# One level of Winograd's scheme in a GEGLU feed-forward kernel: two pairs of f tiles share one run of plain bf16 products

## The chip, the cores and the metric

The kernel runs on one core of one Trainium2 chip. The metric is the device time of one execution in microseconds (us). Three runs of the kernel before took 539.51, 539.78 and 540.17 us; the median is 539.78 us.

TensorE (PE in the profile) multiplies a stationary 128x128 block with a moving 128x512 block and writes to PSUM, which here is used as eight banks of 128x512 f32. VectorE (DVE) and ScalarE (ACT) read and write those banks; GpSimd (POOL) forms sums in SBUF; SyncE (SP) and ScalarE's queue issue the DMAs.

## The reference

```python
B, S, D, F = 1, 2048, 1024, 3584          # all bf16
def reference(x, w_gate, w_up, w_down):
    return (_gelu(x @ w_gate) * (x @ w_up)) @ w_down   # gelu: tanh approximation
```

## The kernel before

The 2048 tokens are done in two halves of 1024. In each half a gate-and-up stage computes `hT`, the transposed product gelu(gate) times up, for all 28 tiles of 128 columns of F; then a down stage multiplies it with `w_down`. A half's tokens are two blocks of 512, held transposed as `xT[0]` and `xT[1]`. This page is about the gate-and-up stage; the down stage (`down_group`, L681) is left as it is.

**Seven products.** Two f tiles form a pair (14 pairs a half). For gate (j = 0) and up (j = 1) each, a pair is a 2x2 block product: weights `a(i, kh)` (f tile i, half kh of D) times x blocks `b(kh, l)` (half kh of D, token block l). Winograd's form needs seven products instead of eight. Two are *plain*: M1 = a(0,0) b(0,0) and M2 = a(0,1) b(1,0), with operands in bf16 straight from the loaded weights and from `xT`. The other five have sums as operands, in fp32r: M5 = s1 t1, M6 = s2 t2, M7 = s3 t3, M3 = s4 b22, M4 = a22 t4. The x sums t1 to t4 are formed once a half (`t_sum`, L241). The weight sums s1 to s4 are formed for every pair, eight of them with gate and up, by POOL (`s_sum`, L364; L385 is the instruction), and `a22` is a cast by ACT (L398). One product is four matmuls (`mm`, L410, instruction at L413), since half of D is four blocks of 128. So a pair is 16 plain matmuls and 40 fp32r ones.

**Banks.** The eight banks are four sets of two (gate and up): PB, VB, QB, RB. M1 goes to one set and ACT copies it to QB (L468); M2 is added to M1 and the pair's first output (f tile 0, tokens 0) is ready: gelu by ACT (`gelu`, L283) and multiplication by DVE (`mult`, L288). M6 is added to the copy of M1 in QB and copied by ACT to RB (L464). M5 goes to the fourth set and is copied by ACT to SBUF (`m5`, L458). DVE adds m5 to QB (`add_m5`, L436), and, when M7 has been added to RB, writes RB plus m5 to M5's set; then M3 is added in QB and M4 in RB. Each of these three sets ends in a gelu and a `mult`.

**Order.** Every engine's order is the order of the program text, fixed by hand (`on`, L110). `pair_quads` (L405) does one pair. It begins with M1; M2 is put on the list `pending` (L403) and is done behind M1 of the *next* pair (L473), so that the plain products of one pair and the next stand together. The last pair of a half does its own M2 at once too. Then come M6, M6, M5, M5 (gate, up each), M7, M3, M4. M1's set alternates between PB and VB (L445). Because M5 of pair p reads s1, and so on, the sums for pair p + 1 are written in place behind the products that read those of pair p (`prep`, L427): POOL starts them when M5 of gate is done, and they are next read by M6 of pair p + 1.

**Work that rides along**, through the dict `then` and the calls of `done`: in the first half, 42 "stage steps" of VectorE (`stage_step`, L619, instruction at L630) form the sums of `w_down` that the down stage needs later and store them to DRAM; each 3 steps need one tile of `w_down` (`stage_load`, L612, three buffers `wd_sb`). Four steps go to a pair: two behind M4's `mult` in DVE's order, and two behind the next M2's `mult`. Also x for the second half is transposed by DMA (`stage_x`, L641), and the next weights, one chunk of gate and one of up for two pairs, are loaded from ACT's queue (`load_w`, L155), gate behind M1, up behind M3. Rows of `w_down` for the down stage are loaded by SP into the weights' memory (`load_wd_rows`, L549, and `load_b22`, L552) at the last two pairs. The DMA semaphores are taken in turn, eight of them, so a DMA also waits until the one eight places before it has landed.

Pair 0 of the first half is done without the scheme (`first_pair_units`, L326); pair 1 of the first half does its M1 and M2 together and forms t4 meanwhile (`eager`, L470).

Of the kernel before, what the change touches and what calls it, by code (L numbers as in the profile page):

```python
# [34 lines left out]
def kernel(  # L35
# [8 lines left out]
    nc = tc.nc  # L44
# [355 lines left out]
    S_NAMES = ("s1", "s2", "s3", "s4", "a22")  # L400


    pending = []  # L403

    def pair_quads(hT, h, pair, nxt, then):  # L405

        key = (h, "p", pair)
        f0 = 2 * pair

        def mm(bank, j, lhs, rhs, start):  # L410
            for c in range(KH):
                pe(
                    nc.tensor.matmul(  # L413
                        banks[bank][:],
                        lhsT=lhs[:, c, :],
                        rhs=rhs[:, c, :],
                        start=start and c == 0,
                        stop=c == KH - 1,
                        skip_group_check=True,
                    )  # L420
                )

        def done(name):
            for f in then.get(name, ()):
                f()

        def prep(j, name):  # L427
            if nxt is not None:
                s_sum(nxt[0], nxt[1], j, name)

        def s(j, name):
            return ssum[(h, pair, j, name)]

        def add_m5(dst, src):
            dve(
                nc.vector.tensor_tensor(  # L436
                    out=banks[dst][:], in0=banks[src][:], in1=m5[j][:], op=ALU.add
                )
            )

        b11 = xT[0][:, half(0), :]
        b21 = xT[0][:, half(1), :]
        m5 = [None, None]
        g = {}
        P_, V_ = (PB, VB) if pair % 2 == 0 else (VB, PB)  # L445

        def m2():
            for j in range(2):
                mm(P_[j], j, block(key, j, 0, 1), b21, False)
                if j == 0:  # L450
                    g[0] = gelu(banks[P_[0]], nxt is None)
                else:
                    mult(hT, g[0], banks[P_[1]], f0, 0)

        def do_m5(j):
            mm(V_[j], j, s(j, "s1"), tsum["t1"], True)
            m5[j] = m_pool.tile([P, TB], F32, name=f"m5_{j}")
            act(nc.scalar.copy(out=m5[j][:], in_=banks[V_[j]][:]))  # L458
            if not eager:
                prep(j, "s1")  # L460

        def do_m6(j):
            mm(QB[j], j, s(j, "s2"), tsum["t2"], False)
            act(nc.scalar.copy(out=banks[RB[j]][:], in_=banks[QB[j]][:]))  # L464

        for j in range(2):
            mm(P_[j], j, block(key, j, 0, 0), b11, True)
            act(nc.scalar.copy(out=banks[QB[j]][:], in_=banks[P_[j]][:]))  # L468
        behind = len(pending) > 0
        eager = not behind and "m2" in then  # L470
        if behind:

            pending.pop()()  # L473
        done("m2 of last")
        if behind:
            if nxt is None:
                m2()
                done("m2")
            else:
                pending.append(m2)  # L480
            order = (do_m6, 0), (do_m6, 1), (do_m5, 0), (do_m5, 1)
        elif eager:
            m2()
            done("m2")
            order = (do_m5, 0), (do_m5, 1), (do_m6, 0), (do_m6, 1)
        else:
            pending.append(m2)
            order = (do_m5, 0), (do_m6, 0), (do_m6, 1), (do_m5, 1)
        for f, j in order:
            f(j)  # L490
            if (f, j) == (do_m6, 1):
                done("m6")
        for j in range(2):
            add_m5(QB[j], QB[j])
            if not eager:
                prep(j, "s2")
        done("m5")
        if eager:
            pool_behind_dve()
            for name in ("s1", "s2"):  # L500
                for j in range(2):
                    prep(j, name)
        for j in range(2):
            mm(RB[j], j, s(j, "s3"), tsum["t3"], False)
            add_m5(V_[j], RB[j])
            prep(j, "s3")
            if j == 0:
                g[1] = gelu(banks[V_[0]], nxt is None)
            else:
                mult(hT, g[1], banks[V_[1]], f0 + 1, 1)  # L510
        done("m7")
        for j in range(2):
            mm(QB[j], j, s(j, "s4"), tsum["b22"], False)
            prep(j, "s4")
            if j == 0:
                g[2] = gelu(banks[QB[0]], nxt is None)
            else:
                mult(hT, g[2], banks[QB[1]], f0, 1)
        done("m3")
        for j in range(2):  # L520
            mm(RB[j], j, s(j, "a22"), tsum["t4"], False)
            prep(j, "a22")
            if j == 0:
                g[3] = gelu(banks[RB[0]], nxt is None)
            else:
                mult(hT, g[3], banks[RB[1]], f0 + 1, 0)

        done("m4")

    SEQ = ("t1", "t2", "t3", "b22", "t4")
# [345 lines left out]

    for h in range(NH):
        hT = hT_pool.tile([P, KF, SH], BF16, name="hT")
        first_pair = 0
        if h == 0:
            first_pair_units(hT)
            first_pair = 1
            xs = [(tb, kd) for tb in (1, 0) for kd in range(KD)]
            new_x(1)
            stage_load(0)  # L890
            stage_load(1)
        for pair in range(first_pair, NPAIR):
            then = {}
            if pair % PPG == 0 and (pair // PPG + 1) * PPG < NPAIR:
                key = (h, pair // PPG + 1)

                if key not in chunks:
                    new_chunk(key)
                    for j, at in enumerate(("m2 of last", "m3")):
                        then[at] = [lambda j=j: load_w(key, j, 0, KD, act)]  # L900
            if h == 0 and pair < PPG:
                then = {
                    "m2": [lambda j=j: s_sum(0, pair, j, "a22") for j in range(2)]
                    + [lambda: t_sum("t4", 0, KH // 2)],
                    "m5": [lambda: t_sum("t4", KH // 2, KH)],
                }
            if h == 0 and pair >= PPG:

                n = [min(4 * (pair - PPG + d), NSTEP) for d in range(3)]
                steps = [lambda k=k: stage_step(k) for k in range(n[0], n[1])]  # L910
                new = range((n[1] + 2) // 3, (n[2] + 2) // 3)

                then["m2 of last"] = (
                    then.get("m2 of last", [])
                    + steps[:2]
                    + [lambda q=q: stage_x(hT, *q) for q in xs[:2]]
                )
                then["m7"] = [store_x] + [lambda i=i: stage_load(i) for i in new]
                then["m4"] = steps[2:]
                xs = xs[2:]  # L920
            if pair == NPAIR - 2:

                then.setdefault("m2 of last", []).extend(
                    [lambda: load_wd_rows(0, 4), lambda: load_wd_rows(4, 8)]
                )
            if 6 < pair < 11:
                i = 2 * pair - 8
                then.setdefault("m6", []).append(
                    lambda i=i: s_down(hT, 0, "s3", i, i + 2)
                )  # L930
            if pair == NPAIR - 1:
                then |= {
                    "m2 of last": [
                        lambda: load_b22(4, NS),
                        lambda: early.append(
                            wd_pool.tile([P, WDT, D], BF16, name="wd_sb")
                        ),
                        lambda: s_down(hT, 0, "s3", 0, 4),
                    ],
                    "m6": [  # L940
                        lambda: s_down(hT, 0, "s1", 4, 8),
                        lambda: t_down(0, "t1", 4, 6),
                    ],
                    "m2": [
                        lambda: load_wd_rows(8, 10),
                        lambda: load_wd_rows(10, 12),
                        lambda: load_wd_rows(12, NS),
                        lambda: load_b22(0, 4),
                    ],
                    "m7": [lambda: s_down(hT, 0, "s1", 0, 4)],  # L950
                    "m3": [lambda: t_down(0, "t1", 0, 2)],
                    "m4": [
                        lambda: t_down(0, "t2", 0, NT2),
                        lambda: t_down(0, "t1", 2, 4),
                        lambda: t_down(0, "t1", 6, 8),
                        lambda: s_down(hT, 0, "s1", 8, NS),
                        lambda: t_down(0, "t1", 8, NS),
                    ],
                }
            pair_quads(  # L960
                hT, h, pair, (h, pair + 1) if pair + 1 < NPAIR else None, then
            )

        then0 = {"m5": [lambda: s_down(hT, 0, "s3", 4, 6)]}
        then1 = {}
# [75 lines left out]
```

## Time and profile before

| what | value |
|---|---|
| median of three runs | 539.78 us |
| span of the profiled execution, first to last instruction | 538.0 us |
| median less span (work around the span) | 1.8 us |
| PE busy | 532.4 us, 99% of the span |
| DVE busy | 364.2 us, 68% |
| ACT busy | 263.5 us, 49% |
| POOL busy | 244.4 us, 45% |
| granted TensorE clock | full in every slice |
| gate and up, first half | about 19.6 to 183.2 us |
| gate and up, second half | about 271 to 447 us |
| one pair in the steady part | 12.56 us |

Busy time is the union of an engine's instructions. Matmuls overlap each other in the records (one lasts 0.38 to 0.39 us, and the next starts some 0.22 us later), so the pace is read from starts, not from durations. Of each run of plain products one record is missing (15 of 16 are listed).

### The profile page before, as it was taken

How to read it: one execution, taken by the hardware profiler on the slowest of the kernel's cores; microseconds unless marked ns; L12 is line 12 of the kernel's file. 1: busy time of each engine (PE TensorE's matmuls, PEld its weight loads, DVE VectorE, ACT ScalarE, POOL GpSimd, SP SyncE). 2: the span in 40 equal slices, each digit the busy share in tenths (PEclk: the TensorE clock that was granted, in tenths of full speed). 3: DMA queues.
4: the chain of work that ended last, by engine and by line, in shares of the span. 5: the costliest groups of instructions: out<-in, count | busy, mean ns of one | idle time of the engine just before them, and what ended most of it. 6: DMA issues, size and time to landing. Idle time of an engine off the chain costs nothing.

```text
span 538.0 us, 7084 instructions
## 1 busy us (share of the span) xinstructions
PE 532.4 (99%) x2352; PEld 377.9 (70%) x2388; DVE 364.2 (68%) x476; ACT 263.5 (49%) x447; POOL 244.4 (45%) x212
## 2 busy tenths in 40 slices
PE   9999999999999999999999999999999999999997
PEld 4577776666776686777776677777777766866866
DVE  1988777788775997989574334444444469969861
ACT  2555555555555329117465555555555552462280
POOL 0699877777776000000056776666777730000000
PEclk9999999999999999999999999999999999999999
DMA  9946876785815977789950405041322448677846
GB/s 205 323 128 195 207 252 185 238 262 197 291 61 200 361 239 246 237 279 308 324 171 1 156 1 158 15 142 57 100 78 80 155 133 284 220 246 252 293 141 212
DMA packets 92547, 102.70 MB, mean 191 GB/s; under 512 B 18656, under 2 KB 67424, under 8 KB 92512
## 3 DMA queue, kind: packets, MB, share of 16 engines
q1 hardware_dynamic: 69568, 80.23, 46.0%
q10 hardware_dynamic: 22944, 22.02, 13.4%
q8 instruction: 19, 0.31, 0.2%
q14 instruction: 16, 0.13, 0.1%
HBM read 85.98 MB, written 12.58 MB: 183 GB/s over the span
## 4 chain that ended last, share of the span: by engine, by line
PE 99%; issue 0%; ACT 0%; ACTq 0%
PE bank L413 63%; PE bank L703 33%; PE bank L264 3%; PE bank L202 1%; PE bank L308 0%; ACT bank L468 0%; ACT o_sb L759 0%; ACTq L468 0%
## 5 line engine op out<-in xcount | busy, mean ns | idle before, releaser
L413 PE MATMUL bank<-t_mem,s_mem 128*128 128x512 f32 x1056 | 249.6, 394 | 0.0
L413 PEld LDWEIGHTS bank<-t_mem,s_mem 128*128 128x128 f32 x1056 | 198.1, 188 | 44.1 <-DVE bank L436 0.4
L385 POOL TENSOR_TENSOR s_mem<-w_mem 128x512 fp32r<-128x512 bf16 x102 | 120.3, 1201 | 190.7 <-DVE t_mem L259 102.8
L703 PE MATMUL bank<-t_mem,s_mem 128*128 128x512 f32 (+1 forms) x548 | 127.2, 391 | 0.0
L288 DVE TENSOR_TENSOR hT<-w_mem,bank 128x512 bf16<-128x512 f32 x104 | 71.3, 687 | 79.9 <-PE bank L413 45.7
L703 PEld LDWEIGHTS bank<-t_mem,s_mem 128*128 128x128 f32 x548 | 102.4, 188 | 22.1 <-issue 0.2
L436 DVE TENSOR_TENSOR bank<-bank,m 128x512 f32<-128x512 f32 x108 | 69.9, 694 | 45.2 <-ACT m L458 43.7
L413 PE MATMUL bank<-xT,w_mem 128*128 128x512 bf16 x405 | 96.5, 380 | 1.4
L283 ACT ACTIVATE w_mem<-bank 128x512 f32<-128x512 f32 x104 | 61.8, 596 | 52.9 <-DVE bank L436 35.8
L413 PEld LDWEIGHTS <-w_mem 128*128 128x128 bf16 x432 | 40.2, 98 | 51.6 <-issue 6.8
L385 POOL TENSOR_TENSOR s_mem<-w_mem,s_mem 128x512 fp32r<-128x512 bf16 x52 | 65.8, 1285 | 0.0
L605 DVE TENSOR_TENSOR t_mem<-w_mem 128x1024 fp32r<-128x1024 bf16 x56 | 65.6, 1219 | 0.0
L385 POOL TENSOR_TENSOR s_mem<-s_mem,w_mem 128x512 fp32r<-128x512 f32 x52 | 60.9, 1192 | 0.0
L464 ACT COPY bank<-bank 128x512 f32<-128x512 f32 x54 | 30.8, 570 | 38.9 <-PE bank L413 38.9
L398 ACT CAST s_mem<-w_mem 128x512 fp32r<-128x512 bf16 x54 | 33.1, 615 | 30.6 <-PE bank L413 29.1
L675 DVE TENSOR_TENSOR s_mem<-hT 128x512 fp32r<-128x512 bf16 x52 | 34.2, 686 | 10.2 <-PE bank L703 9.4
L458 ACT COPY m<-bank 128x512 f32<-128x512 f32 x54 | 31.8, 589 | 17.5 <-PE bank L413 17.5
L703 PEld LDWEIGHTS <-hT 128*128 128x128 bf16 x224 | 21.3, 98 | 26.6 <-issue 2.1
L468 ACT COPY bank<-bank 128x512 f32<-128x512 f32 x54 | 30.7, 570 | 12.7 <-PE bank L413 12.7
L630 DVE TENSOR_TENSOR o_sb<-wd_sb,o_sb 128x512 fp32r<-128x512 bf16 x28 | 31.5, 1126 | 0.5
L768 ACT CAST o_sb<-bank 128x512 bf16<-128x512 f32 x27 | 14.8, 585 | 33.9 <-PE bank L703 33.9
L602 ACT CAST t_mem<-w_mem 128x1024 fp32r<-128x1024 bf16 x28 | 26.9, 1048 | 0.0
(45 smaller groups left out, 238.6 us busy)
## 6 DMA issues: line engine op xcount, KB each, us to landing
t_mem<-t_dram SPq DMA_DIRECT2D x56, 512.0 KB, 5.2
w_mem<-in_w_gate_dram ACTq DMA_DIRECT2D x10, 1024.0 KB, 5.5
w_mem<-in_w_up_dram ACTq DMA_DIRECT2D x10, 1024.0 KB, 5.5
wd_sb<-in_w_down_dram SPq DMA_DIRECT2D x28, 256.0 KB, 4.5
t_dram<-o_sb SPq DMA_DIRECT2D x28, 256.0 KB, 2.4
wd_sb<-in_w_down_dram SPq DMA_DIRECT2D x12, 512.0 KB, 7.7
w_mem<-in_w_down_dram SPq DMA_DIRECT2D x4, 1024.0 KB, 6.6
w_mem<-in_w_down_dram SPq DMA_DIRECT2D x8, 512.0 KB, 8.3
```

The source lines that it names most:

```text
L283: act(nc.scalar.activation(out=g_sb, in_=ps[:], func=ACT.Gelu_apprx_tanh))
L288: nc.vector.tensor_tensor(out=hT[:, fc, tb * TB : (tb + 1) * TB], in0=g_sb, in1=ps[:], op=ALU.mult,)
L385: pool(nc.gpsimd.tensor_tensor(out=t, in0=in0, in1=in1, op=op))
L398: act(nc.scalar.copy(out=t, in_=a(1, 1)))
L413: nc.tensor.matmul(banks[bank][:], lhsT=lhs[:, c, :], rhs=rhs[:, c, :], start=start and c == 0, stop=c == KH - 1, skip_group_check=True,)
L436: nc.vector.tensor_tensor(out=banks[dst][:], in0=banks[src][:], in1=m5[j][:], op=ALU.add)
L458: act(nc.scalar.copy(out=m5[j][:], in_=banks[V_[j]][:]))
L464: act(nc.scalar.copy(out=banks[RB[j]][:], in_=banks[QB[j]][:]))
L605: dve(nc.vector.tensor_tensor(out=t, in0=in0, in1=in1, op=ALU.subtract))
L630: dve(nc.vector.tensor_tensor(out=t, in0=in0, in1=in1, op=ALU.subtract))
L675: dve(nc.vector.tensor_tensor(out=t, in0=in0, in1=in1, op=op))
L703: nc.tensor.matmul(banks[bank][:, c0:c1], lhsT=lhs(i, u), rhs=rhs(i)[:, c0:c1], start=start and i == 0, stop=stop and i == NS - 1, skip_gr ...
```

## The change

`pair_quads` becomes `quads`, which does two pairs (a couple) at a time: M1 of both, then M2 of both, one run of 32 plain matmuls; then the five fp32r products of the first pair, and straight behind them those of the second. `pending` is gone. In the run the first pair uses PB with its copy in QB, the second RB with its copy in VB. After it M5 always goes to PB, RB takes the copy of M6, and M6 and M3 use QB for the first pair and VB for the second. Pair 1 of the first half is alone, in the old order, with VB for M1 and M2.

Of the work that rides along, VectorE's stage steps of a couple go four behind M1, two behind the M2s, one behind M3 of either pair (eight a couple, as before); the place behind M1 is ahead of the M2s' `mult` in VectorE's order. The tiles of `w_down` are loaded as soon as the steps leave a buffer free, at the start of a pair and behind M7, and three of them at first instead of two. Gate weights are loaded behind the M2s instead of behind M1. The order M5, M6, M6, M5 stays for the first couple of the second half alone. The loads of rows 8 to 13 of `w_down` and of the b22 blocks go to the start of the last pair.

```diff
-    def pair_quads(hT, h, pair, nxt, then):
+    def quads(hT, h, members, nxt, thens, m5_first):
+        last = nxt is None
+        run = []
+        for n, pair in enumerate(members):
+            after = (h, members[n + 1]) if n + 1 < len(members) else nxt
+            first_ = (PB, RB)[n] if len(members) > 1 else VB
+            run.append((pair, after, thens[n], first_, (QB, VB)[n]))
...
-        P_, V_ = (PB, VB) if pair % 2 == 0 else (VB, PB)
...
+        for pair, _, _, first_, q_ in run:
             for j in range(2):
+                mm(first_[j], block((h, "p", pair), j, 0, 0), b11, True)
+                act(nc.scalar.copy(out=banks[q_[j]][:], in_=banks[first_[j]][:]))
+        done(0, "m1")
+        for pair, _, _, first_, _ in run:
+            for j in range(2):
+                mm(first_[j], block((h, "p", pair), j, 0, 1), b21, False)
                 if j == 0:
+                    g = gelu(banks[first_[0]])
                 else:
+                    mult(hT, g, banks[first_[1]], 2 * pair, 0)
+        V_, R_ = PB, RB
+        for n, (pair, after, then, _, Q_) in enumerate(run):
...
+            done(n, "start")
+            if eager:
+                order = (do_m5, 0), (do_m5, 1), (do_m6, 0), (do_m6, 1)
+            elif m5_first and n == 0:
+                order = (do_m5, 0), (do_m6, 0), (do_m6, 1), (do_m5, 1)
             else:
+                order = (do_m6, 0), (do_m6, 1), (do_m5, 0), (do_m5, 1)
...
+        def run_steps(n):
+            for k in steps[:n]:
+                stage_step(k)
+            del steps[:n]
+        def run_loads():
+            while loads and 3 * (loads[0] - 2) <= NSTEP - len(steps):
+                stage_load(loads.pop(0))
...
+        for lead in range(begin, NPAIR, PPG):
+            members = range(lead, lead + PPG)
...
+                for j, at in enumerate(("start", "m3")):
+                    add(0, at, lambda j=j, key=key: load_w(key, j, 0, KD, act))
+            if h == 0:
+                add(0, "m1", lambda: run_steps(4))
+                add(0, "start", lambda: run_steps(2))
+                for n in range(PPG):
+                    add(n, "start", run_loads, run_x)
+                    add(n, "m7", store_x, run_loads)
+                    add(n, "m3", lambda: run_steps(1))
...
+                add(
+                    n,
+                    "start",
+                    lambda: load_b22(4, NS),
+                    lambda: load_wd_rows(8, 10),
+                    lambda: load_wd_rows(10, 12),
+                    lambda: load_wd_rows(12, NS),
+                    lambda: load_b22(0, 4),
                 )
...
+            quads(hT, h, members, nxt, thens, lead == 0)
```

## The prediction

> **What bounds the kernel now.** First the page's busy times and the two largest TensorE groups:
>
> ```profile
> PE 532.4 (99%) x2352; PEld 377.9 (70%) x2388; DVE 364.2 (68%) x476; ACT 263.5 (49%) x447; POOL 244.4 (45%) x212
> ...
> L413 PE MATMUL bank<-t_mem,s_mem 128*128 128x512 f32 x1056 | 249.6, 394 | 0.0
> ...
> L413 PE MATMUL bank<-xT,w_mem 128*128 128x512 bf16 x405 | 96.5, 380 | 1.4
> ```
>
> TensorE is never idle in gate and up (0.0 and 1.4 us, the latter beside missing records). The number of matmuls stays the same, so only their pace and new waits of TensorE can move the time. Next, the pace, from TensorE's timeline around three steady pairs (start, length, what, count):
>
> ```profile
> 131.28 3.63 PE L413 MATMUL bank<-xT,w_mem 128*128 128x512 bf16 x15
> 134.55 9.44 PE L413 MATMUL bank<-t_mem,s_mem 128*128 128x512 f32 x40
> 143.84 3.63 PE L413 MATMUL bank<-xT,w_mem 128*128 128x512 bf16 x15
> 147.11 9.44 PE L413 MATMUL bank<-t_mem,s_mem 128*128 128x512 f32 x40
> 156.40 3.63 PE L413 MATMUL bank<-xT,w_mem 128*128 128x512 bf16 x15
> ```
>
> and from two windows of it that lie inside a plain and inside an fp32r run:
>
> ```profile
> 131.94 2.32 PE L413 MATMUL bank<-xT,w_mem 128*128 128x512 bf16 x10
> ```
>
> ```profile
> 136.81 6.51 PE L413 MATMUL bank<-t_mem,s_mem 128*128 128x512 f32 x28
> ```
>
> A pair takes 143.84 - 131.28 = 12.56 us. Inside a run the step is (2.32 - 0.38)/9 = 0.2157 us for a plain matmul and (6.51 - 0.39)/27 = 0.2267 us for an fp32r one. Sixteen and forty make 3.451 + 9.068 = 12.519 us. The remaining **0.041 us is what one change from fp32r to plain and back costs**; no engine's wait is in it. Rounding (0.005 us in 6.51, times 40/27) leaves it between 0.03 and 0.05.
>
> Then the engines that TensorE could have to wait for: GpSimd's and VectorE's timelines.
>
> ```profile
> 137.73 2.29 POOL L385 TENSOR_TENSOR s_mem<-w_mem 128x512 fp32r<-128x512 bf16 x2 [3.07 <-PE bank L413]
> 139.98 2.31 POOL L385 TENSOR_TENSOR s_mem<-s_mem,w_mem 128x512 fp32r<-128x512 f32 x2
> 142.25 2.29 POOL L385 TENSOR_TENSOR s_mem<-w_mem 128x512 fp32r<-128x512 bf16 x2
> 144.50 2.73 POOL L385 TENSOR_TENSOR s_mem<-w_mem,s_mem 128x512 fp32r<-128x512 bf16 x2
> 150.29 2.29 POOL L385 TENSOR_TENSOR s_mem<-w_mem 128x512 fp32r<-128x512 bf16 x2 [3.06 <-PE bank L413]
> ```
>
> ```profile
> 156.84 0.69 DVE L288 TENSOR_TENSOR hT<-w_mem,bank 128x512 bf16<-128x512 f32 x1 [1.30 <-ACT w_mem L283]
> 157.44 1.33 DVE L630 TENSOR_TENSOR o_sb<-wd_sb,o_sb 128x512 fp32r<-128x512 bf16 x1
> 158.69 1.64 DVE L630 TENSOR_TENSOR o_sb<-wd_sb 128x512 fp32r<-128x512 bf16 x1
> 160.26 0.67 DVE L288 TENSOR_TENSOR hT<-w_mem,bank 128x512 bf16<-128x512 f32 x1
> 160.85 1.40 DVE L630 TENSOR_TENSOR o_sb<-wd_sb,o_sb 128x512 fp32r<-128x512 bf16 x2
> ```
>
> GpSimd's eight sums (s1, s2, s3, s4, gate and up) take 9.5 us a pair and end 3.4 us into the next run (144.50 + 2.73 - 143.84). A stage step takes 0.7 us (1.40 for two) where GpSimd rests and 1.33 to 1.64 us where it works.
>
> **The change, part by part.** I lay one couple out from the start of its run, with 0.863 us a plain product and 0.907 us an fp32r one: M1s end at 0.86, 1.73, 2.59, 3.45; M2s at 4.32, 5.18, 6.04, 6.92; the first pair's M6, M6, M5, M5 at 7.83, 8.74, 9.64, 10.55, its M7s at 11.46 and 12.36, M3s at 13.27 and 14.18, M4s at 15.08 and 15.99; the second pair's M6s begin at 15.99 and 16.90, its M5s end at 18.71 and 19.62, its M7s begin at 19.62 and 20.52, its M3s at 21.43 and 22.34; the couple ends at 25.06. ACT starts some 0.25 us behind a product, and its copy takes 0.57, its m5 copy 0.59, its gelu 0.60; DVE's `mult` and `add_m5` take 0.69 (rows of L468, L458, L283, L288, L436).
>
> *Fewer runs.* Before, there is a run for each of 13 pairs of the first half and 14 of the second: 27. After, it is 1 + 6 and 7: 14. Thirteen changes less at 0.041 give **-0.53 us**. Bounds: 0.05 gives -0.65; were the loss tied to the pairs and not to the change of type, 0.
>
> *Banks.* The second pair's M1 writes RB at 1.73 and 2.59; RB's last readers are the gelu and `mult` of the M4s just before. The `mult` row above ends 1.13 us behind the run's start (157.53 - 156.40), and the gelu comes ahead of it: 1.4 us to spare. M2 adds to a bank that is being copied: copy done at 1.73, M2 at 3.45. The copy of M6 (up) into RB must wait for the second M2's `mult`, below. M5 into PB at 8.74 and 9.64 needs the gelu and `mult` of M2s that end at about 5.2 and 6.2. Second pair: the copies of M6 into RB need M4's gelu and `mult` (17.3) and end at 17.8 and 18.6, for M7s at 19.62 and 20.52. Nothing: 0; the least cover is 1.4 us.
>
> *VectorE's steps.* Behind M1 stand four, from 1.04: two beside GpSimd's tail (1.33 + 1.64), two alone (1.40): 5.4 us. The first M2's `mult` could start at 5.43 and is not late (6.1); the second ends at 7.9. Two more steps end at 9.3; m5 is there at 10.5, `add_m5` ends at 11.2 and 12.1, M3 needs it at 12.36 and 13.27. Cover 1.1 us. The first couple is the worst: GpSimd works until 8 us into its run (there the eight sums of pair 2 end at 39.98, the run starts at 32.5), so I charge all four steps 1.64: 7.6, `mult`s at 8.3 and 9.0, two steps to 10.4 to 11.3, `add_m5` 12.0 against 12.36. Still 0. The step behind M3 stands in front of M4's `mult` and costs that 0.7 to 1.6 us, where RB has 3 us. In the second half there are no steps.
>
> *GpSimd.* The second pair follows with no run between. Its s1 can start behind the first pair's M5 (gate), at 9.9; s1, s1, s2 take 2.29 + 1.17 and end at 13.3, and M6 reads s2 at 15.99: **2.7 us of cover, where a run in between left 5.9** (139.98 + 1.17 = 141.2 against the next M6 at 147.11). The fourth ends at 14.5 for 16.90, the last, s4 of up, at 19.4 for 22.34: 2.4 and 2.9 us of cover. For the next couple there are the run's 6.9 us: cover grows.
>
> *Transfers.* Gate weights leave at 7.1 instead of 2.9, up weights at 14.3 instead of 10.1 (issues at 134.14 and 141.37 in the pair of 131.28); they take 5.5 us in the median, so up lands at 20, where the second sum reads it at 20.6. A landing 3 us late moves GpSimd only, which has 6 us until the next M6. ACT's queue blocks while the up issue waits for the DMA eight places ahead, mostly its own gate load (7.1 + 5.5 = 12.6). In the first couple that one is VectorE's sixth step's store, at 11.3 plus 2.4 to 3.7; ACT then has 1 us of idleness ahead of it and RB 1.8 more. SP gets its tile loads in bunches; a tile is issued at about 10 and takes 4.5 us, and the step that first needs it stands at 15.1 or later. The rows 8 to 13 of `w_down` wait for GpSimd's last sums of pair 13, at 19.4, so about 175.8 instead of 173.9; the pieces landed 7.1 to 8.7 us behind issue, so by 184.5 for row 8, and the down stage's first product reads row 8 at 183.2 + 16 x 0.2157 = 186.7. 0, with 2 us of cover.
>
> Sum: -0.53. The profiled span of 538.0 goes to 537.5; the median stands 1.8 us above it, so 539.78 goes to **539.25**.
>
> **A rule against it.** A step beside GpSimd's sum took 1.33 to 1.64 us. The Trainium skill (SBUF — State Buffer, section Who interferes with whom) says that a VectorE instruction with two SBUF inputs and a GpSimd instruction that reads SBUF exclude each other for the whole instruction, so whoever comes second fully blocks. Worked out from that, an estimate by that page: up to 1.16 + 0.7 = 1.86 us a step, 7.4 for four, and the second `mult` ends at about 9.9; the copy that waits for it must begin by 10.8 for M7 at 11.46, so this too stays at -0.53, with less cover.
>
> **Rivals.** *VectorE's burst* (slower). If all six steps run contended at 1.64 us, they and two `mult`s take 1.04 + 9.84 + 1.38 = 12.26, `add_m5` ends at 12.95 and M3 starts 0.6 us late: six couples, 3.6 us, 543 us. It decides once the add ends later than 12.36, which needs GpSimd busy until 9 us; the rows have it end at 3.4. *GpSimd back to back* (slower). If all eight sums of the second pair take 1.60 us, as the one at 158.18 did beside a step, the last is there at 9.9 + 12.8 = 22.7, 0.36 us late, in six couples 2.2 us: 541.5 us; at 2.14, as one at 20.28 us took, it is 4.7 us a couple and 28 in all. It decides from a mean of 1.55 us; the rows show 1.19 with two of eight beside a step, and here one or two are, since VectorE mostly works on banks then. *The loss stays.* If the first fp32r products behind a run are slow because new operands are read, not because the type changes, nothing is saved: 539.8. *More is saved*: faster by over 1.08 us needs 0.083 us a change, twice what the rows hold.
>
> **How the numbers follow.** 0.2% is 1.08 us, about what a measurement here tells from no change. My forecast has 0.68 (538.9 to 539.6 by itself), the loss that stays 0.10 (to 539.9), small waits at seams that I took as covered 0.08 (539.6 to 541, half of it beyond 540.86), the two slower rivals 0.05 each (541 to 544, with a thin tail), more saved 0.04 (below 538.7). So faster 0.04, same 0.82, slower 0.14. The range 538.8 to 540.4 holds the first two cases and a part of the third.
>
> **What would show it.** Right: TensorE's timeline with 32 plain matmuls (one record missing) and 80 fp32r ones, a couple at 25.08 us against 25.12, and no idle time in the fp32r group. Wrong: idle TensorE ahead of M3 ended by VectorE's L431 (the burst), ahead of M6 ended by GpSimd (back to back), ahead of M7 ended by ACT's copy (its queue held up), or a couple at 25.12 (the loss stays).

## The result, and the profile after

The changed kernel takes 541.69 us in the median of six runs (540.78 to 543.51) beside 539.78 us of the kernel before: a ratio of 1.0038, 95% interval [1.0025, 1.0051]. The forecast was 539.25 us, in 538.8 to 540.4. It is slower, by an amount outside the range. Two later timings of the same kernel gave 1.0014 [1.0005, 1.0023] and 1.0030 [1.0020, 1.0041].

In the profiled execution (541.38 us, span 539.6 us), the page's busy times and the same two TensorE groups:

```profile
PE 534.3 (99%) x2388; PEld 378.5 (70%) x2388; DVE 378.2 (70%) x476; ACT 262.8 (49%) x447; POOL 254.1 (47%) x212
...
L415 PE MATMUL bank<-t_mem,s_mem 128*128 128x512 f32 x1056 | 245.3, 392 | 0.8 <-DVE bank L431 0.8
...
L415 PE MATMUL bank<-xT,w_mem 128*128 128x512 bf16 x432 | 95.8, 379 | 0.1
```

The fp32r group now has 0.8 us of idle time ahead of it, ended by VectorE's `add_m5` (L431). VectorE is busy 14 us longer and GpSimd 10 us longer with the same number of instructions: more of their work runs side by side, and there it takes longer (rows below). TensorE's timeline (start, length, what, count, idle time before) over the end of the first half:

```profile
57.86 7.08 PE L415 MATMUL bank<-xT,w_mem 128*128 128x512 bf16 x32
64.59 18.61 PE L415 MATMUL bank<-t_mem,s_mem 128*128 128x512 f32 x80
83.04 7.08 PE L415 MATMUL bank<-xT,w_mem 128*128 128x512 bf16 x32
89.77 18.51 PE L415 MATMUL bank<-t_mem,s_mem 128*128 128x512 f32 x80
108.12 7.08 PE L415 MATMUL bank<-xT,w_mem 128*128 128x512 bf16 x32
114.85 18.51 PE L415 MATMUL bank<-t_mem,s_mem 128*128 128x512 f32 x80
133.20 7.33 PE L415 MATMUL bank<-xT,w_mem 128*128 128x512 bf16 x32
140.17 18.65 PE L415 MATMUL bank<-t_mem,s_mem 128*128 128x512 f32 x80
158.67 7.08 PE L415 MATMUL bank<-xT,w_mem 128*128 128x512 bf16 x32
165.40 14.88 PE L415 MATMUL bank<-t_mem,s_mem 128*128 128x512 f32 x64
180.69 3.91 PE L415 MATMUL bank<-t_mem,s_mem 128*128 128x512 f32 x16 [0.41 <-DVE bank L431]
184.44 1.90 PE L693 MATMUL bank<-w_mem,hT 128*128 128x512 bf16 x8
```

Two couples (83.04 to 108.12 to 133.20) take 25.08 us, as forecast. Three don't: 25.18 (57.86 to 83.04), 25.47 (133.20 to 158.67) and 25.77 (158.67 to 184.44). The last is 0.69 us too long (the profile, which models the ends of matmuls, names 0.41 of it as idle time), and the second half ends in the same way (422.82 to 448.59, 25.77 us, with 0.43 us of named idle time at the same product). This is the sign that the prediction names for *VectorE's burst*, idle TensorE ahead of M3 ended by `add_m5`; here it has another cause.

**Where the last couple waits.** VectorE's and GpSimd's timelines there:

```profile
175.12 0.69 DVE L288 TENSOR_TENSOR hT<-w_mem,bank 128x512 bf16<-128x512 f32 x1 [1.30 <-ACT w_mem L283]
176.55 2.25 DVE L665 TENSOR_TENSOR s_mem<-hT 128x512 fp32r<-128x512 bf16 x2 [0.74 <-POOL s_mem L385]
178.72 1.21 DVE L595 TENSOR_TENSOR t_mem<-w_mem 128x1024 fp32r<-128x1024 bf16 x1
179.86 2.48 DVE L431 TENSOR_TENSOR bank<-bank,m 128x512 f32<-128x512 f32 x4
```

```profile
175.34 2.31 POOL L385 TENSOR_TENSOR s_mem<-w_mem,s_mem 128x512 fp32r<-128x512 bf16 x2
```

Behind M6 of the last pair VectorE forms two s1 sums for the down stage (`s_down`, L665) in the memory where that pair's s2 lies. GpSimd's last s4 of the pair reads s2. Now that no run of plain products stands between the last two pairs, GpSimd forms that s4 at 175.3 to 177.65; VectorE stands idle for 0.74 us with an s1 sum at the head of its queue, that sum then takes 1.64 us beside the last s4 (the other one 0.68), the t1 sum (L595) and the `add_m5` follow late, and M3 waits for the add. In the kernel before, the same sums waited for TensorE alone, since GpSimd had ended 3.4 us earlier (first VectorE, then GpSimd):

```profile
175.34 0.69 DVE L675 TENSOR_TENSOR s_mem<-hT 128x512 fp32r<-128x512 bf16 x1 [0.16 <-PE bank L413]
176.26 0.69 DVE L675 TENSOR_TENSOR s_mem<-hT 128x512 fp32r<-128x512 bf16 x1 [0.23 <-PE bank L413]
```

```profile
169.62 2.28 POOL L385 TENSOR_TENSOR s_mem<-w_mem,s_mem 128x512 fp32r<-128x512 bf16 x2
```

**Where couples of the first half wait.** There are two places. The first is M1 of the next couple. VectorE's timeline of the changed kernel around 133.20:

```profile
132.25 1.58 DVE L620 TENSOR_TENSOR o_sb<-wd_sb,o_sb 128x512 fp32r<-128x512 bf16 x1
133.76 1.64 DVE L665 TENSOR_TENSOR s_mem<-hT 128x512 fp32r<-128x512 bf16 x1
135.32 0.67 DVE L288 TENSOR_TENSOR hT<-w_mem,bank 128x512 bf16<-128x512 f32 x1
```

The last line is the `mult` of the second pair's M4 (up). It stands behind a stage step and an s3 sum, 3.2 us beside GpSimd, and ends at 135.99. The next couple's second M1 (up) writes that bank and should start at 133.20 + 2.59 = 135.79; it starts at 136.05.

The second place is M3 of the first pair, behind the six stage steps at the start of a couple. It shows most in the third timing's profiled execution, in the couple from 132.20 to 157.59 us (VectorE, GpSimd, TensorE):

```profile
136.67 3.09 DVE L620 TENSOR_TENSOR o_sb<-wd_sb,o_sb 128x512 fp32r<-128x512 bf16 x2
...
140.88 1.60 DVE L620 TENSOR_TENSOR o_sb<-wd_sb 128x512 fp32r<-128x512 bf16 x1
142.51 1.54 DVE L620 TENSOR_TENSOR o_sb<-wd_sb,o_sb 128x512 fp32r<-128x512 bf16 x1
143.97 2.48 DVE L431 TENSOR_TENSOR bank<-bank,m 128x512 f32<-128x512 f32 x4
```

```profile
136.05 3.16 POOL L385 TENSOR_TENSOR s_mem<-w_mem 128x512 fp32r<-128x512 bf16 x2
139.17 2.75 POOL L385 TENSOR_TENSOR s_mem<-w_mem,s_mem 128x512 fp32r<-128x512 bf16 x2
```

```profile
138.93 18.82 PE L415 MATMUL bank<-t_mem,s_mem 128*128 128x512 f32 x80
```

GpSimd works until 141.92, 9.7 us into the run, where the prediction has 3.4, and begins the next pair's sums at 142.11; so five of the six steps stand beside its sums and take 1.5 to 1.65 us each. The first add ends at 144.66, 12.46 us into the couple instead of 11.18, and the fp32r run lasts 18.82 us instead of 18.51. In the first profile the same place costs 0.10 us in the couple from 57.86, where the steps began on time, and 0.14 in the one from 133.20.

**Three stretches.** In the 13 profiled executions of this study's changed kernels, which all issue the same instructions up to there, the start of pair 2's run of plain products came anywhere from 31.75 to 33.30 us. That spread of 1.5 us is what makes single executions hard to compare. So I cut each execution at two of TensorE's starts (pair 2's run, the first product of the first down stage) and compare the two stretches behind it:

| kernel | pair 2 starts | to the down stage | to the end | sum of the two |
|---|---|---|---|---|
| before | 32.53 | 150.72 | 354.76 | 505.48 |
| changed | 32.78 | 151.66 | 355.16 | 506.82 |
| changed, second timing | 32.21 | 151.20 | 355.19 | 506.39 |
| changed, third timing | 31.75 | 151.64 | 355.21 | 506.85 |

Forecast for the changed kernel by the price of a change: 150.72 - 6 x 0.041 = 150.47 and 354.76 - 7 x 0.041 = 354.47. The second stretch is 0.69 us over this in the first execution (one last couple), the first 0.69 + 0.50, 0.69 + 0.04 and 0.69 + 0.48.

### The profile page after: what moved, and what is told of

Read it like the earlier page. It is cut to its first block, busy times and chain, and to the rows that moved or that the text cites. A ratio compares the mean times of both kernels' runs of the same rounds, so it can differ in the third digit from the quotient of the medians.

```text
span 539.6 us, 7028 instructions
## 1 busy us (share of the span) xinstructions
PE 534.3 (99%) x2388; PEld 378.5 (70%) x2388; DVE 378.2 (70%) x476; ACT 262.8 (49%) x447; POOL 254.1 (47%) x212
## 4 chain that ended last, share of the span: by engine, by line
PE 94%; DMA 2%; DVE 1%; POOL 1%; issue 1%; POOLq 0%; ACTq 0%; ACT 0%; DVEq 0%
PE bank L415 59%; PE bank L693 33%; PE bank L264 2%; POOL s_mem L385 1%; DMA w_mem<-in_w_up_dram 1%; DMA w_mem<-in_x_dram 1%; DVE t_mem L595 0%; DVE s_mem L665 0%; DVE hT L288 0%; DVE bank L431 0%; POOLq L1053 0%; DVE o_sb L620 0%; ACTq L166 0%; ACT o_sb L749 0%; DVEq L595 0%
## 5 line engine op out<-in xcount | busy, mean ns | idle before, releaser
L415 PE MATMUL bank<-t_mem,s_mem 128*128 128x512 f32 x1056 | 245.3, 392 | 0.8 <-DVE bank L431 0.8
L415 PEld LDWEIGHTS bank<-t_mem,s_mem 128*128 128x128 f32 x1056 | 197.9, 188 | 44.5 <-issue 2.1
L385 POOL TENSOR_TENSOR s_mem<-w_mem 128x512 fp32r<-128x512 bf16 x102 | 126.8, 1263 | 183.8 <-DVE t_mem L259 98.2
L431 DVE TENSOR_TENSOR bank<-bank,m 128x512 f32<-128x512 f32 x108 | 69.5, 693 | 50.4 <-ACT m L469 48.7
L385 POOL TENSOR_TENSOR s_mem<-w_mem,s_mem 128x512 fp32r<-128x512 bf16 x52 | 67.1, 1312 | 3.4 <-PE bank L415 3.4
L595 DVE TENSOR_TENSOR t_mem<-w_mem 128x1024 fp32r<-128x1024 bf16 x56 | 65.6, 1218 | 0.0
L385 POOL TENSOR_TENSOR s_mem<-s_mem,w_mem 128x512 fp32r<-128x512 f32 x52 | 62.9, 1231 | 0.0
L665 DVE TENSOR_TENSOR s_mem<-hT 128x512 fp32r<-128x512 bf16 x52 | 40.6, 812 | 9.7 <-PE bank L693 8.2
L620 DVE TENSOR_TENSOR o_sb<-wd_sb,o_sb 128x512 fp32r<-128x512 bf16 x28 | 35.1, 1254 | 0.5
```

Source lines behind the costliest of these rows:

```text
L385: pool(nc.gpsimd.tensor_tensor(out=t, in0=in0, in1=in1, op=op))
L415: nc.tensor.matmul(banks[bank][:], lhsT=lhs[:, c, :], rhs=rhs[:, c, :], start=start and c == 0, stop=c == KH - 1, skip_group_check=True,)
L431: nc.vector.tensor_tensor(out=banks[dst][:], in0=banks[src][:], in1=m5[:], op=ALU.add)
L595: dve(nc.vector.tensor_tensor(out=t, in0=in0, in1=in1, op=ALU.subtract))
L620: dve(nc.vector.tensor_tensor(out=t, in0=in0, in1=in1, op=ALU.subtract))
L665: dve(nc.vector.tensor_tensor(out=t, in0=in0, in1=in1, op=op))
```

## The experiments

Two causes are to be told apart: the s1 sums of the last pairs (2 x 0.69 us in the profile), and VectorE's and GpSimd's work in the first half (0 to 0.5 us in a profiled execution). And the price of a change of type, from which the gain was worked out, is to be tried by itself.

**The changed kernel again**, with no edit.

> The changed kernel unaltered, profiled a second time. Theory C (last pair: VectorE's s1 sums for the down stage overwrite the memory of s2 and so wait for GpSimd's last s4, and add_m5 and M3 stand behind them): in both halves TensorE again waits 0.6 to 0.7 us ahead of M3 of the last pair, since only the order sets it. Theory A (up weights land late beside the DMA transposes of x, GpSimd is late, VectorE's steps are slowed beside it): the waits in the first half differ from the 0.5 us of the first profile, with landings of the up weights that differ too. Theory B (four steps in a row behind M1, and a step in front of M4's mult, are too much for VectorE in any case): the same waits in the same couples, 0.1 us at the second and 0.4 us at the fifth. Time 540.8 to 543.5 us again.

540.90 us, ratio 1.0014 [1.0005, 1.0023]. All couples of the first half but the last take 25.08 us in this execution, the last 25.79. So the wait of the last pair is there in both executions, and the other waits aren't.

**s1 behind M7.** In the last pair the s1 sums leave the place behind M6:

```diff
                 add(
                     n,
                     "m6",
-                    lambda: s_down(hT, 0, "s1", 4, 8),
                     lambda: t_down(0, "t1", 4, 6),
                 )
-                add(n, "m7", lambda: s_down(hT, 0, "s1", 0, 4))
+                add(
+                    n,
+                    "m7",
+                    lambda: s_down(hT, 0, "s1", 4, 8),
+                    lambda: s_down(hT, 0, "s1", 0, 4),
+                )
```

> In the last pair of each half VectorE's two s1 sums that overwrite s2's memory stand behind M7 instead of behind M6. Theory C: both waits of the last pairs go, 2 x 0.66 = 1.3 us, so about 540.4 us with the first half's waits and their spread of 2 to 3 us left. Rival to C (the wait comes from the late rows of w_down or from add_m5 behind late m5 copies): no change, 541.7 us.

539.58 us, ratio 0.9991 [0.9982, 0.9999]: 1.32 us less than the run above, on the same chip. VectorE's timeline at the end of the first half, and TensorE's:

```profile
176.58 1.36 DVE L595 TENSOR_TENSOR t_mem<-w_mem 128x1024 fp32r<-128x1024 bf16 x1 [0.43 <-PE bank L415]
178.56 0.70 DVE L431 TENSOR_TENSOR bank<-bank,m 128x512 f32<-128x512 f32 x1 [0.62 <-ACT m L469]
...
182.07 2.49 DVE L665 TENSOR_TENSOR s_mem<-hT 128x512 fp32r<-128x512 bf16 x4
```

```profile
159.01 7.08 PE L415 MATMUL bank<-xT,w_mem 128*128 128x512 bf16 x31
165.74 18.51 PE L415 MATMUL bank<-t_mem,s_mem 128*128 128x512 f32 x80
184.09 3.20 PE L693 MATMUL bank<-w_mem,hT 128*128 128x512 bf16 x13
```

The add starts at 178.56, 19.55 us into the couple, as soon as m5 is there; the four sums take 2.49 us alone; the couple takes 25.08. The first cause is settled, and with it gone the kernel is a little faster than the one before, by an interval that only just leaves out no change.

**Up weights loaded with gate.** The suspicion for the first half was that up weights, issued 14.3 us into a couple, land so late that GpSimd works far into the next run beside VectorE's steps. The edit issues them 7 us earlier; the second run below does this and the move of s1 together.

```diff
-                for j, at in enumerate(("start", "m3")):
+                for j, at in enumerate(("start", "start")):
                     add(0, at, lambda j=j, key=key: load_w(key, j, 0, KD, act))
```

> The up weights leave ACT's queue directly behind the gate weights, 7 us earlier in the couple. Theory A: they land before GpSimd's second sum, GpSimd does not wait, the first half's waits go and the spread of the times shrinks below 0.8 us; left is 539.78 - 0.53 + 1.32 = 540.6 us. Theory B: nothing but the landing changes; about 541.7 us, with the same spread and the same waits at the second and fifth couple.

> Both edits: s1 sums behind M7 in the last pair, up weights with the gate weights. Theories A and C: only the saving of the 13 changes between fp32r and plain is left, 539.78 - 0.53 = 539.25 us, with a spread below 0.8 us. Theory B with C: about 540.4 us with a spread of 2 us. If the saving of the changes were not real: 539.8 us.

542.48 us, ratio 1.0040 [1.0028, 1.0052], and with s1 moved too 541.09 us, 1.0018 [1.0009, 1.0026]: 1.5 to 1.6 us worse each time. The remedy made a new wait. VectorE's timeline of the first of the two, then TensorE's:

```profile
125.25 1.14 DVE L620 TENSOR_TENSOR o_sb<-wd_sb 128x512 fp32r<-128x512 bf16 x1 [2.10 <-DMA wd_sb<-in_w_down_dram]
126.31 1.66 DVE L665 TENSOR_TENSOR s_mem<-hT 128x512 fp32r<-128x512 bf16 x1
127.90 0.67 DVE L288 TENSOR_TENSOR hT<-w_mem,bank 128x512 bf16<-128x512 f32 x1
```

```profile
114.70 14.00 PE L415 MATMUL bank<-t_mem,s_mem 128*128 128x512 f32 x60
129.37 5.13 PE L415 MATMUL bank<-t_mem,s_mem 128*128 128x512 f32 x20 [0.68 <-ACT bank L475]
```

The six loads of `w_down` tiles that follow up's 1 MB took 7.7 us in the median instead of 4.7 (the DMA issues in a window around them, against the unaltered changed kernel). The tile of the step behind M3 landed at 125.22; the step stands at the head of VectorE's queue, M4's `mult` behind it, then ACT's copy into that bank, then M7. In the unaltered changed kernel the same tile had landed at 122.12 and its step began at 122.53: 0.4 us of cover. Early, up weights make something else late, and the kernel takes longer. What late up weights cost by themselves this edit can't show: with it GpSimd's sums ended 4.7 us into the next three runs, where they ended 9.4, 8.8 and 5.6 us into them in the first profile, but the new wait hides what that is worth.

**VectorE's steps put into its gaps.** On the kernel with s1 behind M7. The couple's eighth step moves from behind M3 of the second pair to the second pair's start, where VectorE was idle from 17.3 to 19.5 us, and the s3 sums of pairs 7 and 9 move to the last couple's first pair. Nothing stands ahead of the `mult` of the second pair's M4 any more.

```diff
-                    add(n, "m3", lambda: run_steps(1))
+                    add(n, "start" if n else "m3", lambda: run_steps(1))
...
+                if h == 0 and pair == NPAIR - 2:
+                    for i in (6, 10):
+                        add(n, "start", lambda i=i: s_down(hT, 0, "s3", i, i + 2))
-                if 6 < pair < 11:
+                if 6 < pair < 11 and (n == 0 or h > 0):
```

> The changed kernel with s1's second half behind M7 (which took 539.58 us beside 539.96 of the kernel before), and in the first half two more moves of VectorE's work: the eighth step of a couple goes from behind M3 of the second pair to the gap behind M4 of the first pair (VectorE was idle there from 17.3 to 19.5 us into the couple), and the s3 sums of pairs 7 and 9 go from behind M3 of the second pair to the M1s of the last couple. Then nothing stands ahead of the mult of the second pair's M4. Theory 'the second pair's M4 mult is late': the waits of 0.11 us (at 111.25) ahead of the next couple's second M1 are gone from every execution, all couples take 25.08 us, and the time falls by 0.1 to 0.3 us to 539.3 to 539.5. Rival 'the small waits come from something else': they stay, 539.6. Third outcome: the step now comes 5 us earlier, and its tile load may not have landed; then VectorE waits at the second pair's start, add_m5 is late and M3 of the second pair waits, 0.3 us or more a couple: 540 or more.

**x's transposes moved behind M7.** On the kernel with s1 behind M7, in the program's order the second pair's two DMA transposes follow its M7:

```diff
-                    add(n, "start", run_loads, run_x)
-                    add(n, "m7", store_x, run_loads)
+                    add(n, "start", run_loads, *((run_x,) if n == 0 else ()))
+                    add(n, "m7", store_x, *((run_x,) if n else ()), run_loads)
```

> The changed kernel with s1's second half behind M7, and with the two DMA transposes of x that leave at the second pair's start, beside the up load of 14.3 us into the couple, issued behind M7 of the second pair instead, 5 us later. Theory 'the transposes hold the up load up': up lands 5.5 to 7 us behind its issue in the first two couples, instead of 10 to 11, GpSimd no longer waits for it at the first couples' ends, and its tail into the next run shrinks from 9 us to 4 or 5. Rival 'the tile loads beside it, or the up load's own place, do it': 9 to 11 us stay. The time moves little by either: 539.3 to 539.7, since GpSimd's sums have 6 us of cover; that VectorE's steps run alone rather than beside it takes away the small waits only.

**Both of these.**

> Both moves at once, the steps into VectorE's gap and the transposes 5 us later, on the changed kernel with s1's second half behind M7. If both theories hold, no couple has a wait and every one takes 25.08 us: 539.25 us, the forecast of the change itself, 0.7 under the 539.96 of the kernel before. If the steps alone matter: the same as with the steps alone, within 0.1 us. If the transposes, issued behind M7, now delay the tile loads that follow them in SP's queue, a step waits at the head of VectorE's queue, as with the up weights loaded early, and a couple takes 0.3 us or more longer: 540 or more.

> The kernel with all three moves again (s1's second half behind M7, the steps in the gaps, the transposes behind M7), which took 538.92 us beside 539.8 of the kernel before, 0.9 less where the changes of type give 0.53. If that holds: 0.7 to 1.0 us under the kernel before. If part of it was chance: 0.3 to 0.6 under.

The kernel before took 539.96 us beside the first row, 539.80 beside the next three and 539.82 beside the last:

| kernel | median, us | ratio to before | to the down stage | to the end |
|---|---|---|---|---|
| s1 behind M7 | 539.58 | 0.9991 [0.9982, 0.9999] | 150.79 | 354.51 |
| s1 behind M7, steps in gaps | 539.52 | 0.9997 [0.9988, 1.0005] | 150.49 | 354.57 |
| s1 behind M7, transposes later | 539.68 | 1.0005 [0.9990, 1.0019] | 150.70 | 354.45 |
| all three | 538.92 | 0.9984 [0.9976, 0.9993] | 150.49 | 354.49 |
| all three, second timing | 539.10 | 0.9986 [0.9978, 0.9995] | 150.48 | 354.49 |

With the steps in the gaps no profiled execution has a wait between pair 2 and the last couple (five executions, two of them below); with the steps where the change has them, all but one of six have 0.2 to 0.5 us. So the place of the eighth step and of the s3 sums sets both kinds of wait: they make M4's `mult` late, and the next couple's steps then begin up to 1.7 us late and end nearer to M3. Which of the two moves does it isn't told apart; GpSimd's sums also ended earlier in these five executions (7.9 to 9.0 us into the second couple's run instead of 9.3 to 10.2). By the medians the move by itself shows nothing, since 0.3 us is less than the executions differ for other reasons. The move of the transposes by itself tests little: the first eight left as far into their couples as without it (12 to 16 and 13 to 19 us), and up landed 10.8 and 10.9 us behind its issue. With all three moves TensorE's timeline at the end of the first half and its two groups on the page are:

```profile
132.85 7.08 PE L415 MATMUL bank<-xT,w_mem 128*128 128x512 bf16 x32
...
157.93 7.08 PE L415 MATMUL bank<-xT,w_mem 128*128 128x512 bf16 x32
...
183.01 1.25 PE L693 MATMUL bank<-w_mem,hT 128*128 128x512 bf16 x5
```

```profile
L415 PE MATMUL bank<-t_mem,s_mem 128*128 128x512 f32 x1056 | 244.5, 392 | 0.0
...
L415 PE MATMUL bank<-xT,w_mem 128*128 128x512 bf16 x432 | 95.7, 379 | 0.0
```

Every couple takes 25.08 us. The two stretches, 150.48 and 354.49 us, are what the forecast gave, 150.47 and 354.47: their sum is 0.51 us below the kernel before. The medians are 0.88 and 0.72 us below it; whether the rest, 0.2 to 0.4 us, lies in the start of the kernel or is chance the intervals don't say. This version has the two lowest medians of the study.

**One more run of plain products a couple.** The gain was worked out from a price of 0.041 us for a change from fp32r to plain and back. On the kernel with s1 behind M7, the first pair's M6 (gate) is put between the M2s of the two pairs, in all couples but the first of the second half:

```diff
+        split = len(run) > 1 and not m5_first
+        def m6_mm(j):
+            mm(run[0][4][j], ssum[(h, run[0][0], j, "s2")], tsum["t2"], False)
         for pair, _, _, first_, _ in run:
+            if split and pair == run[1][0]:
+                m6_mm(0)
...
             def do_m6(j):
-                mm(Q_[j], s(j, "s2"), tsum["t2"], False)
+                if not (split and n == 0 and j == 0):
+                    mm(Q_[j], s(j, "s2"), tsum["t2"], False)
```

> The changed kernel with s1's second half behind M7, and with the gate product M6 of the first pair put between the M2 products of the two pairs, in all couples but the first of the second half: 12 runs more of plain products, with the same matmuls, the same operands and no work moved to another place. Theory 'each change from fp32r to plain and back costs 0.041 us': a couple without waits takes 25.08 + 0.04 = 25.12 us, TensorE's timeline shows runs of 24 and 8 plain matmuls, and the time is 0.49 us up, 540.07. Rival 'the loss belongs to the pair, or to the stage steps, not to the change of type': couples stay at 25.08 and the time at 539.6. A third outcome is a new wait: the copy of this M6 into its bank must come behind the gelu of the second pair's M2; it would show as idle TensorE ahead of M7, ended by ACT.

540.01 us, ratio 1.0005 [0.9996, 1.0013]. TensorE's timeline of two couples:

```profile
57.38 5.35 PE L415 MATMUL bank<-xT,w_mem 128*128 128x512 bf16 x24
62.38 1.27 PE L415 MATMUL bank<-t_mem,s_mem 128*128 128x512 f32 x4
63.49 1.90 PE L415 MATMUL bank<-xT,w_mem 128*128 128x512 bf16 x8
65.04 17.62 PE L415 MATMUL bank<-t_mem,s_mem 128*128 128x512 f32 x76
82.50 5.35 PE L415 MATMUL bank<-xT,w_mem 128*128 128x512 bf16 x24
...
107.63 0.60 PE L415 MATMUL bank<-xT,w_mem 128*128 128x512 bf16 x2
```

Eleven of the couples take 25.12 or 25.13 us instead of 25.08. Same matmuls, same operands, no pair less or more: the 0.041 us belongs to the change of type. The time by itself would not show it: one couple of the first half (132.75 to 158.26 us) has waits of 0.39 us besides, at the two places described above.

**Transposes held, and s1 moved back.** The changed kernel a third time; the kernel with s1 behind M7 and the steps in the gaps, with the second pair's transposes behind the eighth step, which in the first couple holds two of its four back behind the store of that step; and the version with all three moves but without the move of s1.

```diff
-                    add(n, "start", run_loads, run_x)
                     add(n, "m7", store_x, run_loads)
-                    add(n, "start" if n else "m3", lambda: run_steps(1))
+                    if n == 0:
+                        add(n, "start", run_loads, run_x)
+                        add(n, "m3", lambda: run_steps(1))
+                    else:
+                        add(n, "start", run_loads, lambda: run_steps(1), run_x)
```

and, of the version with all three moves, the s1 sums back where the change has them:

```diff
+                    lambda: s_down(hT, 0, "s1", 4, 8),
                     lambda: t_down(0, "t1", 4, 6),
...
-                    lambda: s_down(hT, 0, "s1", 4, 8),
                     lambda: s_down(hT, 0, "s1", 0, 4),
```

> The changed kernel as it is, beside the three kernels of this call. Two theories of what makes it slow: 'the last pairs' (the s1 sums that overwrite s2 of the last pair of each half, 2 x 0.66 us) and 'VectorE's steps of the first half' (small waits that differ from execution to execution). By both together it is 1.32 us and a few tenths above the kernel that takes both causes away, so 540.4 to 540.9.

> The changed kernel with s1's second half behind M7 and VectorE's steps in the gaps, and in the first couple two of the four DMA transposes of x stand in SP's queue behind the store of the eighth step (51 us) instead of ahead of it (47 us). In the run before this one of the same kernel without that, all four left at 44.6 to 49.7, around the up load of 45.9, which landed 10.5 us behind its issue. Theory 'the transposes hold the up load up': with two of them held, up lands 7 to 8.5 us behind its issue in the first couple, and in the second, where nothing is moved, 10 us as before. Rival 'the tile loads and the load's own place do it': 10 to 11 us in the first couple too. The time stays within 0.3 us of 539.5 by either.

> The changed kernel with the steps in the gaps and the transposes behind M7, but with s1's second half behind M6 of the last pairs, as the change has it. Theory: the two causes are independent and the last pairs cost 2 x 0.66 us whatever the first half does, so it takes 1.3 us more than the kernel with all three moves, about 540.2, and the last couple of each half takes 25.7 to 25.8 us with idle TensorE ahead of M3, ended by VectorE's add. Rival: with VectorE's steps out of the way the add comes early enough and the waits shrink below 0.3 us: 539.4 or less.

The changed kernel: 541.29 us, ratio 1.0030 [1.0020, 1.0041], above the 540.9 that was expected. The transposes held: 539.18 us, 0.9991 [0.9983, 1.0000]; two left at 51.2 and 52.3 us instead of 47.1 and 48.4, and up still landed 10.7 us behind its issue, so that theory falls for these two. Without the move of s1: 540.54 us, 1.0017 [1.0008, 1.0025], 1.44 us more than with it, where 1.3 was expected, and its timeline of VectorE shows the same wait:

```profile
176.52 2.25 DVE L665 TENSOR_TENSOR s_mem<-hT 128x512 fp32r<-128x512 bf16 x2 [0.76 <-POOL s_mem L385]
```

Its last couple is 0.7 us longer, as in the changed kernel, and no other couple is. With s1 moved alone it is the other way round. The two causes are independent.

## Why the prediction was wrong

- **Fewer runs: right.** -0.53 us was forecast; with the new waits gone the two stretches are 0.51 us shorter, and one run more a couple costs 0.04 to 0.05 us again. The rival that the loss stays is refuted.
- **What was left out of the sum: the step that failed.** The sum has no term for VectorE's work in the last pair of a half. Its s1 sums overwrite s2, which GpSimd's last s4 reads. The prediction has GpSimd end at 19.4 us into a couple (it did at 177.65 - 158.67 = 18.98) and asks only when SP's loads that wait for these sums would land. The same number, put beside VectorE's next free moment (175.81 - 158.67 = 17.14), gives the wait. It costs 2 x 0.69 = 1.38 us and turns -0.53 into +0.85, which without any other wait is about 540.6 us and outside the range.
- **"Banks" and "VectorE's steps": the cover was wrong.** "RB has 3 us" holds for the first pair's M4. For the second pair's the text itself gives 1.4 us, from a `mult` row with no step ahead of it. There stand a step (0.7 to 1.6 us) and, in pairs 7 and 9, an s3 sum as well, which the prediction does not list in the first half: 3.2 us. This and the waits at M3 cost 0 to 0.5 us in a profiled execution.
- **"Transfers": sizes wrong, and a consequence left out.** Up weights were to land 5.5 us behind their issue; in the first half they landed 7.3 to 11.1 us behind it in the profiled execution (5.1 to 5.4 in the second half). That a late landing "moves GpSimd only" holds so far as no product ever waited for a weight sum. But GpSimd then worked 5.6 to 9.4 us into the next run, not 3.4, and VectorE's steps stood beside it, most of them at 1.5 to 1.65 us each.
- **The rivals.** *VectorE's burst* came in small: in four of the six executions with the steps where the change has them, M3 of the first pair waited for `add_m5`, by 0.06 to 0.31 us in one or two couples, and not by 0.6 us in all six. Its condition, GpSimd busy until 9 us, was set aside because the rows had it end at 3.4; it was met. *GpSimd back to back* did not come: M6 never waited. Nearest to the result is the case that got 0.08, small waits at seams taken as covered, half of it put beyond 540.86, where the kernel is; but the main wait stands at no seam and in no case of the list, so that the time fell into that case is luck.
- **The rule that was weighed.** The Trainium skill (SBUF — State Buffer, section Who interferes with whom) calls the ports that VectorE shares with GpSimd an exclusive lock; the prediction's estimate from it was up to 1.86 us a step. The rows differ: the longest single step in the profiled executions took 1.73 us, and in the rows above two steps took 3.09 us while two sums beside them took 3.16, where one after the other, at 0.69 and 1.16 us, they would need 3.70. So the trace's figure was the one to use.
- **What remains open.** By their ratios the three timings of the changed kernel are 0.8 to 2.1 us above the kernel before; the two causes give 0.85 to 1.35 in the profiled executions. Each of these was faster than its kernel's median, the third (540.35 us) the fastest of twelve whose slowest took 543.60, so longer waits may stand in executions that no profile shows. The four timings with s1 behind M7 and the steps in the gaps stayed below 540.8 us in 44 executions, while "transposes later", with the steps where the change has them, reached 543.67; that points to VectorE's steps but doesn't show it. The start of the kernel, which varies by 1.5 us, was not examined.

## What to carry to other kernels

When work that separated two phases is taken away, list for every engine the instructions in the narrowed place that *write* memory which another engine still reads, and put the reader's new end beside the writer's new start; the last iteration often carries such extra work, and it is in no steady-state row. Take the cover of a bank from a row with the same instructions ahead of the reader, not from the nearest row of that reader. Before a late transfer is made early, ask which transfers then come behind it and who stands at the head of a queue for them.

## What the runs showed of the hardware

- A change from fp32r to plain bf16 matmuls and back cost TensorE 0.04 to 0.05 us, with all operands there (25.12 and 25.13 us against 25.08 for the same 112 matmuls).
- A VectorE sum of 128x512 with both inputs in SBUF took 0.69 us alone and 1.3 to 1.7 us beside GpSimd's sums, which rose from 1.16 to 1.6 us at the same time.
- The start of the kernel, the same work in all the changed kernels, varied by 1.5 us between executions (pair 2's run at 31.75 to 33.30 us), three times what the change itself was to save.
- One load of 1 MB took from 5.0 to 11.3 us to land, with different transfers under way, and six loads of 256 KB took 7.7 us in the median instead of 4.7 when it was issued ahead of them. What makes the up load slow in the first two couples (10 to 11 us in most executions) stays open: holding two of four transposes until 5.7 us behind its issue did not help (10.7 us), and with the place behind M7 alone they still left at 44.5 to 48.3 us in the first couple, though M7 of the second pair stands at about 52 there: the place in the program set the order of SP's queue, not the time.
